# One table of order for a fused attention and MoE kernel on one Trainium2 core

## The chip, the cores and the metric

The kernel runs on one core of a Trainium2 chip. The metric is the device time of one execution in microseconds (us); a profiled execution also gives a span, from its first to its last instruction. The engines are named as the profile names them: PE (TensorE, matmuls; PEld its weight loads), DVE (VectorE), ACT (ScalarE), POOL (GpSimd), SP (SyncE, here a queue of transfers). POOL and ACT issue transfers too. Each engine works through its own list in order, and waits on semaphores for the others.

## What is computed

```python
# q, k, v: 8 batches, 8 heads, 576 positions, 64 wide; w1, w2: 512 x 1024; w_out: 1024 x 512
scores = scale * np.matmul(q, k.transpose(0, 1, 3, 2))
mask = block_i >= block_j            # blocks of 64 positions
scores = np.where(mask, scores, -1000000000.0)
...
attn = np.exp(scores)
attn = attn / (np.sum(attn, axis=-1, keepdims=True) + 1e-09)
attn_out = np.matmul(attn, v)
x = attn_out.transpose(0, 2, 1, 3).reshape(4608, 512)
h1 = x @ w1
h2 = x @ w2
g = np.maximum(h1, h2)
return g @ w_out
```

## The kernel before

**Attention.** The 64 heads are worked on as 32 pairs; two pairs make a group (16 groups), and two groups a batch. q and k of a group are loaded in fp32 (L121), cast to bf16 (L161), and transposed on PE (L525), with copies out of PSUM (L533). From group 6 on, k takes another way: four casting transfers on POOL's queue (L138) and two transposing transfers on SP (L147). v is loaded with a cast on POOL's queue (L165). Scores of a pair (L544, the causal corner at L562) fill PSUM tiles of 2 x 512, two of them in all; ACT takes the exponential (L568, a corner at L624), POOL writes zeros over masked corners (L573), PE multiplies by v with a column of ones for the sums (L652), and DVE divides (L658, L659). The result goes to `xT`, by PE transposes (L690, L692) for groups 0 to 3 and 15, and by transposing transfers on SP (L670) for the others. For the first four pairs the scores come in smaller pieces (`burst_p`, `burst_q1` to `burst_q3`), so that the first 256 tokens are ready early.

**MoE.** max(h1, h2) is written as h2 + relu(x (w1 - w2)). So g holds relu(x D) with D = w1 - w2 (`diff_w`, L191; `h_unit`, matmul L244, relu L250 on ACT or L252 on DVE), and the output is x M + g w_out with M = w2 w_out (`bT_unit` transposes w2, L261; `m_unit`, L272 and L277). Output tiles of 512 tokens by 512 columns are made as two by two blocks by seven products (`product`, L390; Strassen's scheme in Winograd's form), with sums of the weights (`weight_sums`, L358), sums S1 to S4 of the rows of x and g (`row_sums`, L364: one part of 512 columns from x, one of 1024 from g), and sums of products (`after`, L415 to L449), which stores the output too (L409). All of these sums run on DVE. S1 to S4 lie in one set of buffers, of which the x part alternates with a second set (`xsum`).

Spans of tokens are 256, 320, then 512 each and 448 at the end. Since the first two make 576, later spans start at an odd multiple of 64, and POOL copies the 64 columns of g left over to the next span (L236).

**What sets the order.** The program is written out by hand for the first batch. MoE work is a list of units (`plan`), each with the tokens that it needs and a cost; `fill(n)` takes n units of cost from the first entry that is ready, and the loop over groups calls it between the pieces of attention. `pool_work` places POOL's casts and loads; with `gated=True` a load of q or k is preceded by a memset of one column on POOL (L120), which waits for the buffer in SP's stead. The weights come on POOL's queue, a quarter of w1 and w2 at a time (L185, L187), then w_out in halves (L197). The last span's products go in the order of `LAST` (L390), and `warm_up` issues matmuls on zeros (L514).

Of the kernel before, what the change touches and what calls it, by code (L numbers as in the profile page):

```python
# [14 lines left out]
def kernel(  # L15
# [10 lines left out]
    nc = tc.nc  # L26
# [31 lines left out]
    QCUT = 256  # L58

    def a_col(p, c, t):  # L60
        if p >= HP:
            return CB[c] + t * P
        late = t * P >= QCUT
        return t * P + {
            0: 384 - QCUT if late else 0, 1: 704 - QCUT if late else 256 - P,
            2: 1024 - QCUT, 3: 1408 - 3 * P, 4: 1344 - 4 * P,
        }[c]


    SPAN = 512  # L70
    spans = [(0, QCUT), (QCUT, S - QCUT)]
    spans += [(t0, min(SPAN, NTOK - t0)) for t0 in range(S, NTOK, SPAN)]
    NSPAN = len(spans)


    FAST = 2
    carry = [t0 % P for t0, _ in spans]
    tiles = [(carry[i] + w) // P for i, (_, w) in enumerate(spans)]
# [34 lines left out]
    def load_qk(g, queues, gated=False):  # L113
        b, u = divmod(g, GPB)
        for nm, src, queue in (("q", q, queues[0]), ("k", k, queues[1])):
            if queue is None or by_dma(nm, g):
                continue
            raws[nm, g] = t = raw.tile([P, 2, RPP * D], FP32, name=f"{nm}raw")
            if gated:
                nc.gpsimd.memset(t[:, 0, :1], 0.0)  # L120
            queue.dma_start(  # L121
                out=t[:],
                in_=src[b, 4 * u:4 * u + 4].rearrange(
                    "(s h) (p t) d -> (h p) s (t d)", h=2, t=RPP),
            )

    T_DMA = {nm: 6 for nm in "k"}
    blk_n = {}

    def by_dma(nm, g):  # L130
        return g >= T_DMA.get(nm, NG)

    def load_blocks(nm, g):
        b, u = divmod(g, GPB)
        blk_n[nm, g] = n = raw.tile([P, S // BLK, 2, D], BF16, name=f"{nm}b", tag=f"{nm}raw")
        for h in range(2):
            for s in range(2):
                nc.gpsimd.dma_start(  # L138
                    out=n[h * BLK:(h + 1) * BLK, :, s],
                    in_=(q if nm == "q" else k)[b, 4 * u + 2 * s + h].rearrange(  # L140
                        "(j p) d -> p j d", p=BLK),
                )

    def transpose_blocks(nm, g):
        n = blk_n.pop((nm, g))
        for h in range(2):
            nc.sync.dma_start_transpose(  # L147
                out=(qT_r if nm == "q" else kT_r)[(2 * g + h) % NT].rearrange(
                    "q (j p) -> q j p", p=BLK),
                in_=n[h * BLK:(h + 1) * BLK].rearrange("p j s d -> p (j s d)"),  # L150
            )

    def cast(nm, g, parts):
        if by_dma(nm, g):
            return
        t = raws[nm, g].rearrange("p s (t d) -> p t s d", d=D)
        if (nm, g) not in qk_n:
            qk_n[nm, g] = qkn.tile([P, RPP, 2, D], BF16, name=f"{nm}n")
        n = qk_n[nm, g]
        for copy, j0, j1 in parts:  # L160
            copy(out=n[:, j0:j1], in_=t[:, j0:j1])  # L161
# [19 lines left out]
    def load_w(j, which=(0, 1)):  # L181
        fs = slice(j * WB, (j + 1) * WB)
        if 0 in which:
            w1_raw[j] = wraw.tile([P, NDM, WB], FP32, name="w1raw")
            nc.gpsimd.dma_start(out=w1_raw[j][:], in_=w1r[:, :, fs])  # L185
        if 1 in which:
            nc.gpsimd.dma_start(out=w2_sb[j], in_=w2r[:, :, fs])  # L187

    def diff_w(j):
        fs = slice(j * WB, (j + 1) * WB)  # L190
        nc.vector.tensor_sub(d_sb[:, :, fs], w1_raw[j][:], w2_sb[j])  # L191
# [8 lines left out]
    dve, pool, act = nc.vector.tensor_copy, nc.gpsimd.tensor_copy, nc.scalar.copy  # L200
    SP, ACT = nc.sync, nc.scalar
    warm = small.tile([P, 1], FP32, name="warm")
    load_qk(0, (SP, ACT))
    nc.vector.memset(warm[:], 0.0)
    zeros = wpool.tile([P, SPAN], BF16, name="zeros")
    nc.vector.memset(zeros[:], 0.0)
    nc.scalar.activation(out=warm[:], in_=warm[:], func=AF.Exp)
    load_qk(1, (SP, SP))
    load_qk(2, (SP, None))
    make_identity(nc, ident)  # L210
    for r in range(NV):
        nc.vector.memset(vv_r[r][:, :, :, D:D + 1], 1.0)
        nc.vector.memset(vv_r[r][:BLK, NCH - 1, :, :], 0.0)
    for r in range(NA):
        nc.vector.memset(aT_r[r][:, :, AW:], 0.0)
    for r in range(NT):
        nc.vector.memset(kz_r[r][:, BLK:2 * BLK], 0.0)
    cast("q", 0, ((dve, 0, 7), (pool, 7, RPP)))
    cast("k", 0, ((act, 0, 5), (dve, 5, RPP)))
    for c in range(2):  # L220
        load_v(0, c)
    load_w(0, (0,))
    cast("q", 1, ((pool, 7, RPP),))
    cast("k", 1, ((pool, 0, 7),))
    load_w(0, (1,))


    done_tokens = [0]
    g_tiles = {}

    def h_unit(i, f):
        if f == 0:
            g_tiles[i] = g_pool.tile([P, NFF, SPAN + BLK], BF16, name="g")
            if carry[i]:
                end = carry[i - 1] + spans[i - 1][1]
                nc.gpsimd.tensor_copy(  # L236
                    out=g_tiles[i][:, :, :carry[i]],
                    in_=g_tiles[i - 1][:, :, end - carry[i]:end])
        g = g_tiles[i]
        t0, w = spans[i]  # L240
        m = carry[i]
        pt = ps_m.tile([P, SPAN], FP32, name="ps_h", tag="m")
        for c in range(NDM):
            nc.tensor.matmul(  # L244
                pt[:, :w], d_sb[:, c, f * P:(f + 1) * P], xT[:, c, t0:t0 + w],
                start=(c == 0), stop=(c == NDM - 1),
            )
            if c == NDM - 1:
                if i >= FAST and on_act(i, f):
                    nc.scalar.activation(out=g[:, f, m:m + w], in_=pt[:, :w], func=AF.Relu)  # L250
                else:
                    nc.vector.tensor_scalar_max(g[:, f, m:m + w], pt[:, :w], 0.0)  # L252
                if i in (1, *range(FAST, NSPAN)) and f in X_SUMS:
                    row_sums(i, X_SUMS[f], 0)
            yield

    def bT_unit(j):
        pt = ps_m.tile([P, 2, NDM, P], BF16, name="ps_bT", tag="m")
        for i in range(2):
            for c in range(NDM):  # L260
                nc.tensor.transpose(pt[:, i, c, :], w2_sb[j][:, c, i * P:(i + 1) * P], ident[:])  # L261
                if i == 1 and c == NDM - 1:
                    (act if j % 2 else dve)(
                        out=bT_sb[:, 2 * j:2 * j + 2, :],
                        in_=pt.rearrange("p i c d -> p i (c d)"))
                yield

    def m_unit(i, c):
        ds = slice(i * WH, (i + 1) * WH)
        pt = ps_m.tile([P, WH], FP32, name="ps_M", tag="m")  # L270
        for f in range(NFF):
# [4 lines left out]
            if f == NFF - 1:  # L276
                nc.vector.tensor_copy(out=m_sb[:, c, ds], in_=pt[:])  # L277
                for k in M_SUMS[NDM * (1 - i) + c]:
                    weight_sums(k)
            yield  # L280

    def y_terms(i, s):
        g = g_tiles[i]
        t0 = spans[i][0] - carry[i] + s * P
        return [(xT[:, c, t0:t0 + P], m_sb[:, c]) for c in range(NDM)] + [
            (g[:, f, s * P:(s + 1) * P], wo_sb[:, f]) for f in range(NFF)]

    def y_unit(i, s):
        t0 = spans[i][0] - carry[i] + s * P
        py = ps_m.tile([P, d_model], FP32, name="ps_y", tag="m")  # L290
        terms = y_terms(i, s)
        for n, (lhs, rhs) in enumerate(terms):
            nc.tensor.matmul(
                py[:], lhs, rhs, start=(n == 0), stop=(n == len(terms) - 1),
            )
            if n == len(terms) - 1:
                y = y_pool.tile([P, d_model], FP32, name="y")
                nc.vector.tensor_copy(out=y[:], in_=py[:])
                nc.sync.dma_start(out=out[t0:t0 + P, :], in_=y[:])
            yield  # L300

    def y_last(i, s):
        t0 = spans[i][0] - carry[i] + s * P
        for m, w, copy, queue in ((0, 256, act, SP), (256, P, dve, SP), (384, P, act, ACT)):
            py = ps_m.tile([P, w], FP32, name="ps_y", tag="m")
            terms = y_terms(i, s)
            for n, (lhs, rhs) in enumerate(terms):
                nc.tensor.matmul(
                    py[:], lhs, rhs[:, m:m + w], start=(n == 0), stop=(n == len(terms) - 1),
                )  # L310
                if n == len(terms) - 1:
                    y = y_pool.tile([P, d_model], FP32, name="y")
                    copy(out=y[:, :w], in_=py[:])
                    queue.dma_start(out=out[t0:t0 + P, m:m + w], in_=y[:, :w])
                yield

# [12 lines left out]
    def a_parts(i, row, half):  # L329
        j, r = (row, 0) if i == 1 else (i, row)  # L330
        g, t0 = g_tiles[j], spans[j][0] - carry[j] + 2 * r * P
# [605 lines left out]
```

## Time and profile before

| what | before |
|---|---|
| device time, median of 3 runs | 247.88 us (247.6 to 254.31) |
| device time of the profiled execution | 247.61 us |
| its span | 245.8 us |
| mean granted PE clock | 0.997 |
| busy: PE, DVE, ACT, POOL | 234.4, 185.4, 143.8, 129.6 us |
| first h matmul | 18.6 us |
| first matmul of M, first of the seven products | 38.3 us, 52.2 us |
| last attention matmul | 204.5 us |

Busy time is the union of an engine's instructions. A matmul's record runs from its start until its result is written, so matmuls overlap and a busy PE is not PE at its peak. In the groups, a line gives the line of the kernel, the engine, the operation, output<-inputs and their shape, the count, then busy us and mean ns of one, then idle time ahead of them and what ended it. A few matmul records are missing.

### The profile page before, as it was taken

Reading aid. Unit: us, or ns where it says so; the run is one execution under the profiler, and the core shown is the slowest. Engines: PE = TensorE matmul, PEld = TensorE weight load, DVE = VectorE, ACT = ScalarE, POOL = GpSimd, SP = SyncE. Lnnn points to the kernel's source line nnn. Section 1 sums busy time; section 2 is a strip of 40 time slices with the busy share of each in tenths; the row PEclk is TensorE's granted clock in tenths of the full one; section 3 lists DMA queues with packets and bytes.
Section 4 is the critical chain, followed back from the end, with each engine's and each line's share of the span. In section 5 each row is a group of like instructions: output and inputs, shape, how many; then the busy total and the mean of one; then the engine's idle time right before and its main releaser. Section 6 shows DMA issues by size and latency. Waiting matters only on the chain.

```text
span 245.8 us, 7595 instructions
## 1 busy us (share of the span) xinstructions
PE 234.4 (95%) x3093; PEld 167.3 (68%) x3109; DVE 185.4 (75%) x395; ACT 143.8 (58%) x200; POOL 129.6 (53%) x294
## 2 busy tenths in 40 slices
PE   7689899999999999999999999999999999999993
PEld 2347666688865886588558755875587578567782
DVE  4976989999677958795879587957785788526573
ACT  2888871677677748673867386748673730462200
POOL 1996952669959584948593859485621210010000
PEclk9999999999999999999999999999999999999998
DMA  6999999579999999999999999999994321301125
GB/s 233 318 206 306 231 278 195 172 137 188 153 196 180 168 163 222 184 201 183 244 227 130 208 164 272 122 223 193 134 138 97 100 39 45 131 0 43 47 86 172
DMA packets 108867, 41.33 MB, mean 168 GB/s; under 512 B 89248, under 2 KB 102688, under 8 KB 108832
## 3 DMA queue, kind: packets, MB, share of 16 engines
q0 software_dynamic: 65952, 11.87, 69.4%
q1 hardware_dynamic: 42464, 28.32, 51.7%
q10 hardware_dynamic: 416, 0.66, 0.8%
q8 instruction: 24, 0.39, 0.7%
q14 instruction: 11, 0.09, 0.1%
HBM read 34.60 MB, written 9.44 MB: 179 GB/s over the span
## 4 chain that ended last, share of the span: by engine, by line
PE 87%; DVE 7%; ACT 4%; issue 1%; ACTq 0%
PE ps_p L390 35%; PE ps_h L244 24%; PE ps_o L652 11%; PE ps_s L544 9%; PE ps_w L514 3%; ACT aT L568 3%; PE ps_qT L525 2%; DVE sums L358 2%; DVE sums L364 1%; DVE g L252 1%; DVE m_sb L277 1%; PE ps_s L562 1%; PE ps_xe L690 1%; PE ps_bT L261 1%; DVE qT L533 1%
## 5 line engine op out<-in xcount | busy, mean ns | idle before, releaser
L568 ACT ACTIVATE aT<-ps_s 128x1024 bf16<-128x1024 f32 (+2 forms) x100 | 95.7, 994 | 32.1 <-PE ps_s L544 24.0
L244 PE MATMUL ps_h<-xT,d_sb 128*128 128x512 bf16 (+3 forms) x307 | 68.0, 357 | 1.0 <-DVE d_sb L191 0.3
L573 POOL MEMSET aT<- 64x128 bf16 x124 | 21.8, 200 | 52.8 <-ACT aT L568 51.9
L244 PEld LDWEIGHTS <-d_sb 128*128 128x128 bf16 x320 | 29.7, 98 | 26.7 <-issue 2.2
L652 PEld LDWEIGHTS <-aT 128*128 128x128 bf16 x960 | 37.2, 98 | 6.9 <-issue 0.8
L652 PE MATMUL ps_o<-vv,aT 128*128 128x65 bf16 x960 | 39.8, 194 | 0.3 <-DVE xp L659 0.3
L250 ACT ACTIVATE g<-ps_h 128x512 bf16<-128x512 f32 (+1 forms) x40 | 23.3, 587 | 23.3 <-PE ps_h L244 22.3
L165 POOL DMA_DIRECT2D vv<-in_v_dram x40 | 33.9, 857 | 1.1 <-issue 0.9
L252 DVE TENSOR_SCALAR g<-ps_h 128x512 bf16<-128x512 f32 (+2 forms) x40 | 23.6, 594 | 13.1 <-PE ps_h L244 12.8
L659 DVE TENSOR_TENSOR xp<-ps_o,rec 128x256 bf16<-128x256 f32 (+1 forms) x64 | 31.4, 491 | 2.2
L544 PE MATMUL ps_s<-qT,kT 64*128 64x64 bf16 (+6 forms) x344 | 31.3, 280 | 1.8 <-ACT kT L533 0.7
L390 PE MATMUL ps_p<-sums,bT_sb 128*128 128x256 bf16 x216 | 32.8, 273 | 0.0
L390 PEld LDWEIGHTS <-bT_sb 128*128 128x128 bf16 x288 | 27.5, 98 | 4.5 <-issue 1.4
L138 POOL DMA_DIRECT2D kb<-in_k_dram x40 | 29.5, 765 | 0.0
L533 ACT COPY qT<-ps_qT 128x576 bf16<-128x576 bf16 (+1 forms) x17 | 10.3, 614 | 23.2 <-PE ps_qT L525 23.2
L390 PEld LDWEIGHTS <-g 128*128 128x128 bf16 x220 | 19.8, 98 | 4.8 <-issue 2.8
L390 PE MATMUL ps_p<-wo_sb,g 128*128 128x256 bf16 (+1 forms) x148 | 22.7, 270 | 0.0
L161 POOL CAST qn<-qraw 128x1152 bf16<-128x1152 f32 (+1 forms) x16 | 17.1, 1067 | 5.1 <-DMA qraw<-in_q_dram 5.1
L544 PEld LDWEIGHTS <-kT 64*128 64x128 bf16 x344 | 12.2, 94 | 10.5 <-issue 5.1
L658 DVE RECIPROCAL rec<-ps_o 128x4 f32<-128x4 f32 (+1 forms) x64 | 11.8, 184 | 6.8 <-PE ps_o L652 6.8
L236 POOL COPY g<-g 128x512 bf16<-128x512 bf16 x8 | 5.9, 733 | 20.6 <-ACT g L250 20.3
L364 DVE TENSOR_TENSOR bT_sb<-g 128x1024 bf16<-128x1024 bf16 x18 | 12.4, 688 | 5.4 <-ACT g L250 4.8
(90 smaller groups left out, 326.1 us busy)
## 6 DMA issues: line engine op xcount, KB each, us to landing
qraw<-in_q_dram SPq DMA_DIRECT2D x16, 576.0 KB, 6.0
out_dram<-y SPq DMA_DIRECT2D x35, 256.0 KB, 3.9
vv<-in_v_dram POOLq DMA_DIRECT2D x32, 128.0 KB, 7.3
kraw<-in_k_dram SPq DMA_DIRECT2D x5, 576.0 KB, 7.4
kb<-in_k_dram POOLq DMA_DIRECT2D x40, 72.0 KB, 6.8
w1raw<-in_moe_w_dram POOLq DMA_DIRECT2D x4, 512.0 KB, 8.8
xT<-in_moe_w_dram POOLq DMA_DIRECT2D x4, 256.0 KB, 9.2
wo_sb<-in_moe_w_out_dram POOLq DMA_DIRECT2D x2, 512.0 KB, 10.9
```

The source lines that it names most:

```text
L138: nc.gpsimd.dma_start(out=n[h * BLK:(h + 1) * BLK, :, s], in_=(q if nm == "q" else k)[b, 4 * u + 2 * s + h].rearrange("(j p) d -> p j d", ...
L161: copy(out=n[:, j0:j1], in_=t[:, j0:j1])
L165: nc.gpsimd.dma_start(out=vv_r[b % NV][P - rows:, c, :, :D], in_=v[b, :, c * P:c * P + rows, :].rearrange("h p d -> p h d"),)
L244: nc.tensor.matmul(pt[:, :w], d_sb[:, c, f * P:(f + 1) * P], xT[:, c, t0:t0 + w], start=(c == 0), stop=(c == NDM - 1),)
L250: nc.scalar.activation(out=g[:, f, m:m + w], in_=pt[:, :w], func=AF.Relu)
L252: nc.vector.tensor_scalar_max(g[:, f, m:m + w], pt[:, :w], 0.0)
L390: nc.tensor.matmul(pt[:, q0:q0 + w], lhs[c][:, s * P:(s + 1) * P], rhs[c][:, m:m + w], start=(c == 0 and q0 == 0), stop=(c == 5 and q0 + w ...
L544: nc.tensor.matmul(ps[:, hh, col:col + w], kT[r, k0:k0 + P], qT[r, q0:q0 + w], start=True, stop=True,)
L568: nc.scalar.activation(out=aT_r[p % NA][:, :, a0:a0 + w], in_=ps[:, :, :w], func=AF.Exp, scale=scale,)
L573: (eng or nc.gpsimd).memset(aT_r[p % NA][BLK:, :, a0:a0 + BLK], 0.0)
L652: nc.tensor.matmul(po[:, gi, hh, :], a[:, hh, a0:a0 + P], vv[:, c, h0 + 2 * hh, :], start=(mm == 0), stop=(mm == n_mm - 1),)
L659: nc.vector.tensor_mul(xp[:, :, ts[0]:ts[0] + n, p % 2].rearrange("q s t d -> q t s d"), po[:, :, :, :D], rec[:, :n].to_broadcast([P, n, 2 ...
```

## The change

The order is no longer made while the program is built: a table of some 950 tokens is read from the front, and each token issues one step (`step`). `S4_2` is score tile 2 of pair 4; `E4_2:P` its exponential with the masks on POOL; `A4a`/`N4a` the AV product and its division, first (a) or second (b) part; `Cq3a:P` a cast; `Tq3`, `cq3_1:D` transposes and a copy out; `Lq3`, `u0`, `v0`, `o0` loads of q, w1, w2, w_out; `K6_0`, `J6_0`, `I4_0`, `V1_3` the k and x transposing ways and v; `B`, `M`, `D`, `W` the steps of the weights; `R5_21:P` row sum S2 of span 5, part 1 (g); `H4` four h matmuls, `Y4` eight matmuls of products. The letter after the colon names the engine.

- Spans: nine of 512 tokens, each by the seven products; the left-over copy of g and `xsum` are gone.
- All scores of all pairs are made in full tiles (three of 512 columns), where the first four pairs had smaller pieces.
- w2, w_out and M come ahead of w1; w1 is loaded on SP's queue. The loads of q and k on SP have a gate only where the table names an engine (`Lk2:P`, `Lk3:P`, `u0:D`, `Lq10:P`).
- The engine of each cast, copy, mask and sum is chosen in the table. All four `diff_w`, three of eight `weight_sums` and 40 of 72 `row_sums` go to POOL (21 of the 40 are of 1024 columns, 19 of 512); 64 of 128 masks go to DVE, and several casts and copies change between POOL, DVE and ACT.
- The division (`normalize`) is a step of its own and may come later than the AV product.
- PE's list changes from 3109 to 3069 matmuls; the warm-up matmuls are 29 in both.

```diff
-    spans = [(0, QCUT), (QCUT, S - QCUT)]
-    spans += [(t0, min(SPAN, NTOK - t0)) for t0 in range(S, NTOK, SPAN)]
-    NSPAN = len(spans)
+    NSPAN = NTOK // SPAN
...
-    def load_w(j, which=(0, 1)):
-            nc.gpsimd.dma_start(out=w1_raw[j][:], in_=w1r[:, :, fs])
+    def load_w1(j, gate=None):
+        w1_raw[j] = t = wraw.tile([P, NDM, WB], FP32, name="w1raw")
+        if gate is not None:
+            gate.memset(t[:, 0, :1], 0.0)
+        nc.sync.dma_start(out=t[:], in_=w1r[:, :, j * WB:(j + 1) * WB])
...
-    def diff_w(j):
-        nc.vector.tensor_sub(d_sb[:, :, fs], w1_raw[j][:], w2_sb[j])
+    def diff_w(j, eng):
+        eng.tensor_sub(d_sb[:, :, j * WB:(j + 1) * WB], w1_raw[j][:], w2_sb[j])
...
-    def row_sums(i, n, k):
+    def row_sums(i, n, k, eng):
+        sums_slots()
+        sub, add = eng.tensor_sub, eng.tensor_add
...
-        for m in G_SUMS.get(n, ()):
-            row_sums(i, m, 1)
...
+    SCHEDULE = """
+        z14 mk:D mz2:P Cq0a:P V0_2 ma:D Ck0a:A V0_1 V0_3 Cq0b:D Tq0 Ck0b:A mo1:D Lq1:N Cq1a:A Tk0 ck0_1:A
+        ck0_0:D cq0_1:A cq0_0:D z6 S0_1 V0_0 V0_4 Z1 S1_1 Lk1:N Ck1a:D Ck1b:A Z0 Tk1 ck1_0:D v2 z2 S0_0 E1_1:P
...
+        E2_1:D B1:D S3_0 E3_0:P X0:DA S2_2 E2_2:P B2:D B0:D A2a N2a B3:A Lk2:P A3b A2b Lq2:N A3a u0:D Lk3:P
+        Ck2a:P M02:A M00:A N2b M01:A Ck2b:A N3a N3b X1:AD Cq2a:P M12:D D0:P M11:D Tk2 ck2_0:D Z4 Cq2b:A u1:N
+        u2:N ck2_1:A D1:P Z5 V1_3 M03:D D2:P Tq2 cq2_0:A M13:A Ck3a:A Ck3b:D H2 Lq3:N Cq3a:P H1 M10:A cq2_1:D
...
+        S16_1 Tq9 H1 cq9_0:A H4 A13b K10_2 H4 Y5 V4_3 N13b I6_1 Y1 A15a
...
+        Y1 R7_21:P R7_40:D Y5 H3 Y4 H4 Y2 H2 R7_41:D H1 Y1 H1 Y5 H1 Y5 H1 Y4 H5 R8_11:D Y1 R8_30:D Y5 R8_31:P
+        Y2 R8_10:P R8_20:P R8_40:D Y4 R8_21:P Y4 R8_41:D Y32
+    """
...
+        elif kind == "D":
+            diff_w(n[0], ENGINE[o])
+        elif kind == "R":
+            row_sums(n[0], *divmod(n[1], 10), ENGINE[o])
+        elif kind == "H":
+            for _ in range(n[0]):
+                next(h_work)
+        elif kind == "Y":
+            for _ in range(2 * n[0]):
+                next(y_work)
```

## The prediction

> **What bounds the kernel now.** I read the page's first two parts, then busy time by stage, then the chain of waits, then the groups of POOL by shape, then the timeline and the DMA issues. From the page and its slices:
>
> ```profile
> span 245.8 us, 7595 instructions
> PE 234.4 (95%) x3093; PEld 167.3 (68%) x3109; DVE 185.4 (75%) x395; ACT 143.8 (58%) x200; POOL 129.6 (53%) x294
> PE   7689899999999999999999999999999999999993
> POOL 1996952669959584948593859485621210010000
> ```
>
> By stage (start:end, length, then busy us and count of each engine, granted clock, DMA):
>
> ```profile
> 6.00:24.00 18.00, 14.74 (x287) 9.03 (x287) 14.02 (x34) 14.73 (x23) 15.47 (x29) 1.00 1.43 277
> 36.00:72.00 36.00, 35.03 (x590) 27.25 (x591) 33.05 (x72) 21.78 (x29) 22.92 (x54) 1.00 1.32 169
> 72.00:190.00 118.00, 117.53 (x1575) 83.44 (x1582) 89.48 (x184) 77.84 (x105) 76.38 (x176) 1.00 1.66 184
> ```
>
> PE leaves 0.5 of 118 us idle from 72 us on; what it loses, it loses before. The chain of waits gives its price per matmul:
>
> ```profile
> 207.09 3.38 PE ps_p L390 x30
> 210.95 7.18 PE ps_h L244 x33
> ```
>
> In the dense stretches the timeline has a matmul start every 0.109 us (256 columns), 0.216 (512), 0.056 (128), 0.029 (65, attention times values); products over 64 rows run in pairs, at half of that each; a change from 128 rows to 64 costs 0.096 and back 0.085. Priced so, all of PE's list is 227.0 us before and 226.8 us after the change. It is a good price: from 71.5 us to the last matmul the list says 168.0 us, the trace took 170.0. So the span is 1.2 (first matmul) + 227.0 + 13.4 lost + 4.2 (last sum and store), and 11.4 of the 13.4 are lost before 71.5 us. Only those can be won, and anything that stops PE later is a loss.
>
> **The change part by part, with no cost of its own.** Nine equal spans in place of 256, 320, seven of 512 and 448 tokens, and full score tiles: PE's price falls by 0.2 us, eight POOL copies of g (0.73 each) go, 16 exponentials of the first four pairs become 12: all beside PE. Masks, casts and q/k copies change engine; DVE, ACT and POOL keep idle time in each stage above. w1 goes from POOL's queue to SP's: four issues fewer on POOL, 3.1 us in all. Loads of q on SP lose their gate, so SP itself waits for the buffer, with output stores and transposes queued behind; with three buffers per tensor that buffer was cast three groups earlier (a group takes 12 us in the chain), so I cost it at nothing.
>
> **The head, up to the first h matmul.** It needs w1's first quarter, loaded after w2 and w_out. On ACT: the casts of k0 end at 7.6 (first row of ACT 6.25, 0.73 and 0.6), then one cast of q1, two copies (0.64 each) and one cast of k1: 10.3. Then twelve exponentials of four pairs, which the timeline shows at 3.46 us for four, so 0.9 each, with four short ones and a copy: the twelfth ends at 23. POOL masks it, and only then issues the gate memset for group 2's loads on SP; w1's first quarter is third there, at 24.5. From before:
>
> ```profile
> 21.48 3.46 ACT L568 ACTIVATE aT<-ps_s 128x1024 bf16<-128x1024 f32 x4
> ...
> w1raw<-in_moe_w_dram POOLq DMA_DIRECT2D x4, 512.0 KB, 8.8
> wo_sb<-in_moe_w_out_dram POOLq DMA_DIRECT2D x2, 512.0 KB, 10.9
> ```
>
> So it lands at about 33 (24.5 + 8.8). PE meanwhile has, from 25.5, the last three AV tiles, M (eight matmuls a unit, 0.87 us) and transposes, 9 us: 34.5, if w_out (issued at 17, 10.9 to land: 28) is there soon enough. First h at 35. What is left on PE's list: 288 h 62.2, 762 product matmuls 82.4, 840 AV 24.4, scores 19.2, transposes 5.0, one M 0.9, 45 changes of rows 8.1: 202.1. Without any stop: 35 + 202.1 + 4.2 = 241.3, against 245.8. The head's gain is 4.5 us, because M fills idle PE time.
>
> **What it adds: POOL as a second adder.** Before, every row sum, weight sum and w1 - w2 runs on DVE. After, POOL gets the four w1 - w2, three weight sums, and 40 of 72 row sums. No row of before shows POOL adding two tensors. Its nearest rows have one input:
>
> ```profile
> L165 POOL DMA_DIRECT2D vv<-in_v_dram x40 | 33.9, 857 | 1.1 <-issue 0.9
> L138 POOL DMA_DIRECT2D kb<-in_k_dram x40 | 29.5, 765 | 0.0
> L573 POOL MEMSET aT<- 64x128 bf16 x124 | 21.8, 200 | 52.8 <-ACT aT L568 51.9
> L161 POOL CAST qn<-qraw 128x1152 bf16<-128x1152 f32 x14 | 16.2, 1160 | 0.6 <-DMA qraw<-in_q_dram 0.6
> L551 POOL COPY kz<-kT 128x128 bf16<-128x128 bf16 x28 | 8.9, 340 | 8.2 <-DMA qraw<-in_q_dram 6.2 <-DMA kT<-kb 1.1
> L161 POOL CAST qn<-qraw 128x256 bf16<-128x256 f32 x2 | 0.8, 417 | 4.5 <-DMA qraw<-in_q_dram 4.5
> ```
>
> The two casts give 0.83 ns an element and 0.2 us fixed. Low end: a second input is free, 1.05 us for 1024 and 0.63 for 512. High end: each input is read at the cast's rate, 1.9 and 1.05. I take the high end: a POOL that needs 0.83 ns for one stream shows no spare reading, and the next rows show POOL and DVE in each other's way as soon as DVE has two inputs. The same sum of 512 columns took 0.41 alone and 0.96 beside a POOL cast, until that cast ended:
>
> ```profile
> 148.76 0.96 DVE L364 TENSOR_TENSOR xsum<-xsum,xT 128x512 bf16<-128x512 bf16 x1
> 149.64 0.41 DVE L364 TENSOR_TENSOR xsum<-xT 128x512 bf16<-128x512 bf16 x1
> ...
> 148.29 1.15 POOL L161 CAST qn<-qraw 128x1152 bf16<-128x1152 f32 x1
> ```
>
> [...]
>
> **Where POOL stops PE.** POOL's list is in order, and its first w1 - w2 can't start before the load lands, 33. From there to the cast of q for group 9, which PE's transposes wait for, it holds: 17 v loads 14.6, 19 k loads 14.5, 14 key pads 4.8, 27 masks 5.4, 9 casts 9.1, small 0.7, together 49.0; and 9 sums of 1024 and 6 of 512. Low: 49.0 + 9 x 1.05 + 6 x 0.63 = 62.3, done at 95.3. High: 49.0 + 17.1 + 6.3 = 72.4, done at 105.4. PE's own price from first h to those transposes is 59.3, so it is there at 94.3. Hold: 1.0 low, 11.2 high. Before that point the casts of q and k for group 5 and a row sum of span 0 pass part of it on; after it POOL's list is lighter than PE's, and nothing more is held until the ends of the late spans. There POOL's sums stand right ahead of their readers:
> - Span 6: from the last h, PE has 2.7 us up to the sixth product's use of S2; the relu (0.7) and two POOL sums of 1024 follow each other. High 4.5, stop 1.8; low 0.1.
> - Span 7: 4.9 us for relu, 1024, 512, 1024. High 5.6, stop 0.7; low none.
> - Span 8: S3's buffer comes free at span 7's last product; POOL then does 1024, 512, 512, 1024 before the sixth product can go on, with two products (2.8 us) on PE in between. High 5.9, stop 3.1; low 3.4, stop 0.5. Before, DVE did these with no loss on PE.
>
> Together high 5.6, low 0.6. Sum: 241.3 + 11.2 + 5.6 = 258.1 us of span. The profiled execution took 247.61 for a span of 245.8, so 1.8 more: 259.9, **260 us**. It agrees with the median 247.88 of the runs to 0.1%.
>
> **Rivals.** (1) POOL's second input is free: 241.3 + 1.0 + 0.6 + 1.8 = 244.7, within 2% (a difference under 2% is about what a measurement of this kernel can't tell from no change). For it: POOL is idle 47% of the span. Against it: the cast's rate. (2) The other sign, faster: M ahead of h fills the head, and POOL holds nothing. It needs sums of 1024 at about 1 us and w1's first quarter 2 us earlier, as the fastest w1 load of before (8.05 to 14.49, 6.4 us) would have it: first h at 33, 239.3 of span, 241.1, 2.7% faster. It decides where h starts before 35 and POOL's list to group 9 takes under 61 us. Against it: behind w2, w_out and two loads of group 2 the queues are full. (3) The change doesn't fill the head: w_out's second half took 12.9 us to land in before (25.19 to 38.08), and now v and w2 are in front of it; M starts at 30 instead of 25.5 and h at 39. By itself that is 4 us on rival 1: 249, no change. With POOL at the high end POOL hides it.
>
> **How the numbers follow.** POOL at the high end or beyond 0.63, its own range 252 to 268 (a price between the ends at the bottom; at the top each POOL sum also waits for a DVE sum). Rival 1 and rival 3 together 0.22, at 243 to 250. Rival 2: 0.15. All of the first case but its top, and rivals 1 and 3 from 242 up, make the range 242 to 268, leaving out rival 2 and a little above. Faster by over 2% 0.15, within 2% 0.22, slower 0.63.
>
> **What would show it.** In the profile after: the mean of POOL's TENSOR_TENSOR of 1024 (1.9 expected; 1.05 is rival 1); first h matmul at 35; POOL over 90% busy from 35 to 105 and PE's idle time there ended by POOL (qn, kn, sums); in the last 12 us PE stops for about 3 us ahead of the sixth product. Wrong: POOL's sums near 1 us with PE dense from 50 us on, or PE stopped by DMA, DVE or ACT instead.

## The result: 284.1 us, 14% slower, and the profile after

The changed kernel took 284.1 us (median of 4 runs, 282.93 to 284.54), the kernel before 248.8 beside it: a ratio of 1.144 [1.136, 1.152]. Ratios leave out executions over 1.5% above the fastest of their kernel, such as the one of 254.31 us of the kernel before. The profiled execution took 282.93 us, its span is 281.2. So the direction of the forecast came true, and its size did not: 36 us were lost (over the 247.88 of the kernel before that the prediction used), not 12.

From the page of the changed kernel, the span, the busy times, and the slices of PE, POOL and the granted clock:

```profile
span 281.2 us, 7430 instructions
PE 241.7 (86%) x3043; PEld 163.2 (58%) x3069; DVE 179.0 (64%) x393; ACT 150.9 (54%) x211; POOL 183.8 (65%) x254
PE   8689783889987887999999999999899779989573
POOL 3950499999994899798929916966564660560720
PEclk9999999999999999999999999999999979999978
```

PE no longer has its unbroken row of nines. POOL is at nine tenths or more from 35 to 84 us. And in two slices near the end, both 7, the granted clock is below full (the last slice, an 8, is below full in the kernel before too); the PEclk row of the kernel before has a 9 in every slice but the last.

By stage, with the columns as before (start:end, length, busy us and count of PE, PEld, DVE, ACT, POOL, then clock, DMA share, GB/s):

```profile
6.00:24.00 18.00, 14.79 (x271) 9.29 (x273) 12.07 (x32) 16.31 (x23) 12.12 (x22) 1.00 1.38 175
36.00:72.00 36.00, 28.81 (x457) 18.43 (x458) 30.07 (x57) 25.10 (x35) 35.00 (x45) 1.00 1.04 175
72.00:190.00 118.00, 107.75 (x1391) 71.99 (x1404) 81.42 (x189) 72.47 (x99) 90.82 (x139) 1.00 1.42 163
```

From 36 to 72 us PE does 457 matmuls where it did 590, and POOL has 1 us free of 36. From 72 to 190 us PE has 10 us idle where it had 0.5.

POOL's costliest groups, each shape apart:

```profile
L262 POOL TENSOR_TENSOR bT_sb<-g 128x1024 bf16<-128x1024 bf16 x9 | 19.6, 2176 | 19.5 <-PE ps_p L282 10.6 <-ACT g L187 5.4 <-issue 1.9
...
L262 POOL TENSOR_TENSOR sums<-xT 128x512 bf16<-128x512 bf16 x11 | 12.9, 1172 | 11.6 <-PE ps_p L282 11.0 <-POOL aT L423 0.2
...
L161 POOL TENSOR_TENSOR d_sb<-w1raw,xT 128x1024 bf16<-128x1024 f32 x4 | 8.5, 2131 | 2.1 <-DMA w1raw<-in_moe_w_dram 2.0
```

A sum of 1024 columns takes POOL 2.12 to 2.18 us and one of 512 takes 1.15 to 1.17 (means of the groups): a little over the high end of the prediction (1.9 and 1.05), three times DVE's 0.69 and 0.41 in the kernel before. The 47 sums take POOL 81.3 us in all.

The waits say who stops PE (engine, line, waited for: us in total, times, longest):

```profile
PE ps_p L282 <- POOL bT_sb L262: 6.8, 3, 3.8
...
PE ps_h L181 <- DVE g L189: 4.6, 2, 2.7
...
PE ps_qT L376 <- POOL qn L131: 3.1, 4, 1.6
...
DVE sums L262 <- POOL sums L262: 3.1, 2, 2.0
...
PE ps_p L282 <- POOL sums L262: 2.6, 1, 2.6
...
DVE sums L254 <- POOL d_sb L161: 1.9, 1, 1.9
```

POOL stops PE itself, and it stops DVE, which stops PE. (Among the waits left out here, PE waits 2.8 us for loads of v, in three stops.) How the second works is seen in the timeline of the changed kernel, from 42 us (start, length, instruction, and in brackets the idle time ahead and its releaser):

```profile
42.08 0.91 DVE L254 TENSOR_TENSOR sums<-sums,m_sb 128x512 bf16<-128x512 bf16 x1 [1.93 <-POOL d_sb L161]
...
42.91 0.68 DVE L189 TENSOR_SCALAR g<-ps_h 128x512 bf16<-128x512 f32 x1
...
43.64 1.02 PE L181 MATMUL ps_h<-xT,d_sb 128*128 128x512 bf16 x4 [1.82 <-DVE g L189]
44.19 2.13 POOL L161 TENSOR_TENSOR d_sb<-w1raw,xT 128x1024 bf16<-128x1024 f32 x1
...
44.93 1.94 DVE L254 TENSOR_TENSOR sums<-wo_sb 128x1024 bf16<-128x1024 bf16 x1
46.27 1.80 POOL L135 DMA_DIRECT2D vv<-in_v_dram  x2
46.79 1.37 DVE L254 TENSOR_TENSOR sums<-m_sb 128x512 bf16<-128x512 bf16 x1
...
48.08 0.68 DVE L189 TENSOR_SCALAR g<-ps_h 128x512 bf16<-128x512 f32 x1
...
48.81 0.38 PE L181 MATMUL ps_h<-xT,d_sb 128*128 128x512 bf16 x1 [2.74 <-DVE g L189]
```

A weight sum on DVE first waits 1.93 us for POOL's w1 - w2 (the sums lie in the buffers that w1 was loaded into). Two more take 1.94 and 1.37 us where alone they take 0.67 and 0.41, the first beside POOL's sum, the second beside POOL's DMA issues. The relu stands behind them in DVE's list, and PE behind the relu: 1.8 and 2.7 us.

To see where time is lost I use the prediction's price list: the *lateness* of a matmul is its start less the price of all matmuls ahead of it on PE's list. It grows only where PE waits or runs slower. All variants of the changed kernel have the same list on PE, so they can be compared point by point:

| lateness, us | predicted | after | all sums on DVE | one copy on POOL | copies on DVE |
|---|---|---|---|---|---|
| first h matmul (price 24.9) | 10.1 | 10.8 | 12.2 | 10.0 | 12.1 |
| first q transpose of group 9 (83.9) | 21.5 | 28.7 | 21.4 | 18.1 | 20.0 |
| last matmul (226.8) | 27.1 | 49.8 | 35.7 | 24.3 | 28.5 |

The last three columns are experiments 1, 2 and 5 below. The kernel before ends 14.6 late by its own list.

### The profile page after: what moved, and what is told of

It is laid out like the page before. It is cut to its first block, busy times and chain, and to the rows that moved or that the text cites. A ratio compares the mean times of both kernels' runs of the same rounds, so it can differ in the third digit from the quotient of the medians.

```text
span 281.2 us, 7430 instructions
## 1 busy us (share of the span) xinstructions
PE 241.7 (86%) x3043; PEld 163.2 (58%) x3069; DVE 179.0 (64%) x393; ACT 150.9 (54%) x211; POOL 183.8 (65%) x254
## 5 line engine op out<-in xcount | busy, mean ns | idle before, releaser
L418 ACT ACTIVATE aT<-ps_s 128x1024 bf16<-128x1024 f32 x96 | 95.1, 1025 | 26.3 <-PE ps_s L394 24.9
L181 PE MATMUL ps_h<-xT,d_sb 128*128 128x512 bf16 x265 | 70.9, 380 | 8.6 <-DVE g L189 4.6
L187 ACT ACTIVATE g<-ps_h 128x512 bf16<-128x512 f32 x40 | 24.0, 599 | 54.8 <-PE ps_h L181 50.3
L282 PE MATMUL ps_p<-sums,bT_sb 128*128 128x256 bf16 x216 | 35.6, 284 | 6.8 <-POOL bT_sb L262 6.8
L262 POOL TENSOR_TENSOR bT_sb<-g 128x1024 bf16<-128x1024 bf16 x9 | 19.6, 2176 | 19.5 <-PE ps_p L282 10.6
L394 PE MATMUL ps_s<-qT,kT 64*128 64x512 bf16 (+4 forms) x320 | 31.4, 288 | 1.0 <-ACT aT L418 0.7
L189 DVE TENSOR_SCALAR g<-ps_h 128x512 bf16<-128x512 f32 x32 | 22.0, 686 | 13.0 <-PE ps_h L181 13.0
L423 POOL MEMSET aT<- 64x128 bf16 x64 | 11.6, 205 | 26.8 <-ACT aT L418 25.6
L282 PE MATMUL ps_p<-sums 128*128 128x256 bf16 x108 | 21.9, 286 | 3.4 <-POOL sums L262 2.6
L475 DVE RECIPROCAL rec<-ps_o 128x4 f32<-128x4 f32 (+1 forms) x64 | 11.7, 183 | 14.9 <-PE ps_o L464 14.4
L262 POOL TENSOR_TENSOR sums<-xT 128x512 bf16<-128x512 bf16 x11 | 12.9, 1172 | 11.6 <-PE ps_p L282 11.0
L282 PEld LDWEIGHTS <-sums 128*128 128x128 bf16 x144 | 13.6, 101 | 8.8 <-POOL sums L262 3.4
L394 PEld LDWEIGHTS <-kT 64*128 64x128 bf16 x320 | 11.2, 94 | 10.1 <-issue 7.6
```

What stands on the lines that cost most here:

```text
L181: nc.tensor.matmul(pt[:], d_sb[:, c, f * P:(f + 1) * P], xT[:, c, t0:t0 + SPAN], start=(c == 0), stop=(c == NDM - 1),)
L187: nc.scalar.activation(out=g[:, f], in_=pt[:], func=AF.Relu)
L189: nc.vector.tensor_scalar_max(g[:, f], pt[:], 0.0)
L262: op(s_parts(i, n)[k], get(x)[k], get(y)[k])
L282: nc.tensor.matmul(pt[:, q0:q0 + w], lhs[c][:, s * P:(s + 1) * P], rhs[c][:, m:m + w], start=(c == 0 and q0 == 0), stop=(c == 5 and q0 + w ...
L394: nc.tensor.matmul(ps[:, hh, col:col + w], kT[r, k0:k0 + P], qT[r, q0:q0 + w], start=True, stop=True,)
```

## Experiments

The ratios are to the kernel before on the same chip, which took 247.7 to 247.8 us.

**1. All 47 sums to DVE.** The theory was the prediction's: POOL is the cause. The rival: the order of the table is.

```diff
-  D0:P ... R0_10:P ... W6:P ... R8_21:P      (47 tokens)
+  D0:D ... R0_10:D ... W6:D ... R8_21:D
```

> All 47 two-input sums that the table gives to POOL (w1 - w2, weight sums, row sums) are done by DVE instead; the order of the table stays. POOL theory (POOL's price for a sum, 2.1 us against DVE's 0.7, is what holds PE): nearly all of the 35 us comes back, 246 us (242 to 252), no stop of PE ended by a sum, the granted clock without a slow stretch after 10 us. Rival, order theory (the table's order itself makes PE wait for DVE, ACT and loads, whoever adds): half comes back at most, 262 us or more.

268.9 us, 1.083 [1.079, 1.087]: 15 us come back of 36. POOL's theory fails by its number (246). The rival's number holds (262 or more), but it does not show the order alone at fault, since DVE now has 47 more sums: ahead of products PE waits 6.5 us for DVE's sums, in eight stops. From 36 to 72 us DVE is busy for 33.62 of 36 us. The kernel before had 33.05 there with PE idle for 1 us, so a full DVE by itself is not the reason; what stands ahead of the relus and copies that PE needs is.

```profile
36.00:72.00 36.00, 31.92 (x473) 20.87 (x475) 33.62 (x70) 27.27 (x38) 24.81 (x44) 0.96 1.28 188
```

**2. Each POOL sum a copy of its first input.** The instructions and their places stay; the second input, the arithmetic and a wait for the second input alone are left out (S4 is A - S2, so a copy of A no longer waits for S2). The same edit is made for w1 - w2.

```diff
+        one = lambda o, a, b: eng.tensor_copy(out=o, in_=a)
+        sub, add = (one, one) if eng is nc.gpsimd else (eng.tensor_sub, eng.tensor_add)
```

> POOL's 47 sums are replaced by POOL copies of their first input alone, so that the second input is left out of the sums; all else is as in the changed kernel. POOL theory: the copy takes 1.1 us for 1024 columns instead of 2.1, POOL is about 31 us less busy, and the time falls by two thirds of what was lost, to 252 us (247 to 260); DVE's sums still wait beside it. Order theory: 270 us or more.

258.5 us, 1.043 [1.038, 1.048]. The copies take about half, on POOL's rows of this kernel:

```profile
L259 POOL COPY bT_sb<-g 128x1024 bf16<-128x1024 bf16 x15 | 16.1, 1079 | 20.1 <-PE ps_p L284 13.9 <-ACT g L187 4.1 <-issue 1.9
...
L259 POOL COPY sums<-xT 128x512 bf16<-128x512 bf16 x13 | 8.2, 638 | 10.9 <-PE ps_p L284 10.5
```

All 47 together take 41.4 us of POOL instead of 81.3, and the execution is 25.6 us shorter. So the second input, with what waits for it, costs 25.6 of the 36 us. But this is also the case that the first rival of the prediction assumed (1.05 and 0.63), and it priced it at 244.7.

**3. The 15 POOL sums of the last three spans to DVE** (tokens `R6_10:P` to `R8_21:P`).

> Only the row sums of spans 6, 7 and 8 move from POOL to DVE (15 of them). POOL theory: the three stops ahead of the sixth products (4.0, 1.5 and 4.6 us) and the two slow stretches of the clock after them (1.7 us each) go, 13 us together: 271 us. Order theory: DVE, which has the sums of products as well, makes PE stop in their place, and less than 5 us comes back.

276.4 us, 1.113 [1.108, 1.118]: 7.7 us come back, between the two theories (13, and less than 5). In their place PE now waits 4.9 us in four late stops for DVE's sums.

**4. w1 - w2 and the weight sums to DVE** (`D0` to `D3`, `W5` to `W7`).

> Only the four w1 - w2 and the three weight sums move from POOL to DVE. POOL theory: PE's lateness between the first h matmul and the first AV of pair 4 (7.3 us) shrinks by 4 us, of which the later hold of POOL's list takes none back, since POOL's list gets 14 us shorter before group 9: 275 us (270 to 280). Order theory: no change, 284 us, or slower since DVE stands in front of the relus of span 0.

280.7 us, 1.131 [1.126, 1.136]: 3.4 us come back, again between the two (9, and none). The first h matmul then starts at 37.2 instead of 35.6, since DVE waits 3.23 us for w1 with copies of M behind.

After these four, two theories were left: that the rest is still the sums, by their place right ahead of their readers; or that the order of masks, casts and loads costs by itself.

**5, 6 and 7. How much the table costs without dear sums.** In 5, all weight and row sums are copies of their first input, on DVE, and w1 - w2 is a true subtraction there; in 6, all masks are on POOL besides; in 7, the sums are true sums on DVE, as in 1, with all masks on POOL.

```diff
-        op(s_parts(i, n)[k], get(x)[k], get(y)[k])
+        nc.vector.tensor_copy(out=s_parts(i, n)[k], in_=get(x)[k])     (5 and 6)
...
-  E0_1:D ... E30_2:D        (6 and 7: 49 tokens)
+  E0_1:P ... E30_2:P
```

> The changed kernel, with every weight sum and row sum replaced by a copy of its first input, on DVE (the second input and the arithmetic are left out; w1 - w2 stays a subtraction, on DVE). The order of all else is the table's. Sum theory (what the table loses, 36 us, it loses at the sums, on whichever engine they stand): PE loses about what it lost in the kernel before: 246 to 251 us. Table theory (loads, casts, masks and copies in the table's order stop PE by themselves): not under 255 us, since copies on POOL gave 258.5.

> As the kernel with every sum a copy of its first input on DVE (the second input is left out), and all masks on POOL besides. Mask theory: 3 to 6 us less than that kernel. Sum theory: the same as it within 1.5 us. If both theories fall, it stays over 255 us, and loads (v, k) or the table's order on PE are what is left.

> The changed kernel with all 47 two-input sums on DVE, and all masks on POOL, which the sums leave free (as in the kernel before). Mask theory (49 score tiles have their masks on DVE, which waits there 13.8 us for exponentials with relus, copies and sums queued behind): 258 to 264 us, against 268.9 with the masks as in the table. Sum theory (DVE is full of sums where PE waits, masks are idle time that costs nothing): 267 to 270 us.

261.5 us, 1.053 [1.048, 1.059]; 267.0 us, 1.079 [1.074, 1.084]; 272.4 us, 1.098 [1.094, 1.102]. The sum theory's number (246 to 251) fails in the first: with copies of 0.3 to 0.5 us in the place of all sums the table still loses 14 us. That does not clear the sums of all of it. PE still waits 3.5 us in four stops for these copies, and 2.5 us at 34.7 for a copy of M that stands behind w1 - w2 on DVE; PE's granted clock is 0.50 from 34.0 to 40.8, which costs up to 3.0 us more. The mask theory fails with the wrong sign (3 to 6 us less in 6, 258 to 264 us in 7 were forecast): masks on POOL cost 5.4 us more (6 against 5) and 3.5 more (7 against 1). A mask waits for its exponential, and on POOL the casts, loads of v and key pads wait behind it; in the second of the three kernels PE's waits for masks are 3.0 us in three stops. In the kernel before, with its masks on POOL, PE is idle 0.5 us of 118.

**8. The test from the other side: the kernel before with the change's 40 row sums on POOL.**

```diff
+        if (i, n, k) in ON_POOL:        # the 40 of the table
+            op = nc.gpsimd.tensor_add if n == 1 else nc.gpsimd.tensor_sub
         op(s_parts(i, n)[k], get(x)[k], get(y)[k])
```

> The kernel before, with the 40 row sums that the change gives to POOL run on POOL, and nothing else changed. Price theory (a two-input sum of 2.18 us on POOL, and DVE sums that wait beside it, cost PE wherever they are placed): all 47 sums were worth 15 us in the changed kernel, the seven of the weights 3.4 of them, so some 12 us here too: 260 us (255 to 266). Place theory (only the table's place for them, right ahead of their readers, makes them cost; before's list has slack, POOL is idle 47% of its span): 248 to 251 us.

284.8 us, 1.149 [1.146, 1.153]: 37 us from the sums alone, in an order that had lost 2 us after 72 us. Both theories fail (260; 248 to 251). That it is as much as the change lost is chance: there 11 us of the loss are left with cheap sums (2), and here part of it is the clock, which was granted at 0.50 for 23.9 us in four stretches that begin in stops or behind them (up to 9 us, for the 17.6 us of it in which PE has work). The timeline of this kernel shows one of its stops from the start:

```profile
79.24 1.15 POOL L161 CAST qn<-qraw 128x1152 bf16<-128x1152 f32 x1
80.32 2.43 POOL L165 DMA_DIRECT2D vv<-in_v_dram  x3
...
82.73 2.96 POOL L138 DMA_DIRECT2D kb<-in_k_dram  x4
85.63 1.23 POOL L366 TENSOR_TENSOR sums<-sums,xT 128x512 bf16<-128x512 bf16 x1
86.89 0.42 DVE L366 TENSOR_TENSOR sums<-xT,sums 128x512 bf16<-128x512 bf16 x1 [6.50 <-POOL sums L366]
...
87.92 0.66 PE L536 MATMUL ps_qT<-ident,qn 64*128 64x64 bf16 x17 [5.93 <-DVE xp L670]
```

S4 on DVE needs S2 from POOL. POOL first casts and issues seven loads (6.5 us), so DVE waits 6.50 us for a sum of 1.23. The division stands behind DVE's sum, PE's transposes wait for the PSUM buffer that the division reads: 5.93 us. Two more stops of this kind are 5.29 and 3.82 us, where DVE waits 5.86 and 7.00 us for a POOL sum; and PE itself waits 5.8 us in four stops for POOL's sums of 1024.

**9. Nine POOL sums that no other sum waits for.** The kernel before with only the x part of S3 on POOL.

```diff
+        if (n, k) == (3, 0):
+            op = nc.gpsimd.tensor_sub
```

> The kernel before, with one row sum of each span on POOL: the 512 columns of x in S3, which no other sum reads. Place theory (with 40 sums on POOL the kernel before lost 37 us because DVE's sums wait for POOL's, S2 for S1 and S4 for S2, with the division behind them): 247 to 250 us, no loss. Price theory (each us of POOL sum costs its share: 9 x 1.17 us of the 40 sums' 68 us): 253 us (251 to 256).

248.0 us, 0.9995 [0.995, 1.004]: free. PE's line on this kernel's page is that of before, and its POOL sums take no less than elsewhere:

```profile
PE 234.6 (95%) x3093; PEld 167.2 (68%) x3109; DVE 184.0 (75%) x386; ACT 143.8 (58%) x200; POOL 140.7 (57%) x303
...
PE   7689899999999999999999999999999999999993
```

```profile
L366 POOL TENSOR_TENSOR sums<-xT 128x512 bf16<-128x512 bf16 x5 | 6.4, 1273 | 0.3
...
L366 POOL TENSOR_TENSOR xsum<-xT 128x512 bf16<-128x512 bf16 x4 | 5.0, 1260 | 0.2
```

So it is not a price per microsecond of POOL: a sum of 1.26 us with slack ahead of its reader costs nothing. The nine differ from the forty of experiment 8 in their readers, but in their number and length too; which of these made them free is not shown.

**10. Is it POOL's time or what the instruction does to DVE?** Each POOL sum of the changed kernel as two copies, one per input.

```diff
+        two = lambda o, a, b: (eng.tensor_copy(out=o, in_=b), eng.tensor_copy(out=o, in_=a))
+        sub, add = (two, two) if eng is nc.gpsimd else (eng.tensor_sub, eng.tensor_add)
```

> The changed kernel with each of the 47 two-input sums on POOL replaced by two copies, one of each input (the arithmetic is left out). POOL is then as long at each of them as in the changed kernel (1.06 x 2 for 1024 columns, 0.63 x 2 for 512, from the kernel with one copy), but never reads two inputs at once. Time theory (what costs is that POOL is late, whatever its instruction is): 280 to 286 us, like the change. Lock theory (what costs is that DVE's sums can't run beside POOL's, 0.41 to 0.69 us become 1.9 to 2.3): 268 to 274 us.

282.6 us, 1.141 [1.135, 1.147]. The 94 copies take POOL 83.1 us (81.3 for the sums), and the time is that of the change. One copy 258.5, two copies 282.6, the sum 284.1: what counts is how long POOL takes at these places, not that one of its instructions reads two inputs. The lock (DVE's sums taking longer beside POOL) is not parted from it by this: DVE's sums still take longer beside the copies (0.82 us in place of 0.98 for the seven `sums<-xT,sums`, 0.41 alone).

**11. DVE's own 37 sums as copies of one input, POOL's as they are.**

```diff
+        one = lambda o, a, b: eng.tensor_copy(out=o, in_=a)
+        sub, add = (eng.tensor_sub, eng.tensor_add) if eng is nc.gpsimd else (one, one)
```

> The changed kernel with the 37 row and weight sums that the table gives to DVE replaced by copies of their first input (the second input and the arithmetic are left out), POOL's sums as they are. Lock theory: DVE no longer waits beside POOL, its relus and copies come on time from 36 to 60 us, where 5 us of PE's stops were ended by a relu: 270 to 277 us. Time theory: POOL is as late as before, 279 to 284 us.

280.6 us, 1.134 [1.127, 1.141]. By its numbers it speaks for time, but it does not tell what it was made to tell: the copies on DVE wait beside POOL as well. The timeline of this kernel:

```profile
43.71 2.11 POOL L161 TENSOR_TENSOR d_sb<-w1raw,xT 128x1024 bf16<-128x1024 f32 x1
43.75 2.37 DVE L249 COPY sums<-wo_sb 128x1024 bf16<-128x1024 bf16 x1
45.78 1.80 POOL L135 DMA_DIRECT2D vv<-in_v_dram  x2
46.03 1.67 DVE L249 COPY sums<-m_sb 128x512 bf16<-128x512 bf16 x1
```

Copies that take 0.42 and 0.28 us alone (experiment 5) took 2.37 and 1.67. How many microseconds the lock is worth in the change stays open.

**12. Sums on DVE, only w1 - w2 left on POOL** (tokens `R` and `W` to DVE).

> The changed kernel with the row sums and weight sums on DVE, and only the four w1 - w2 left on POOL. If what the version with all 47 on DVE paid at its head is DVE waiting for w1 with M's copies queued behind (PE stopped 2.2 us there, and the clock fell to a half for 3.4 us after it): first h matmul at 35.5 instead of 37.0, no half clock at 36, 264 to 267 us. If not: 268 to 270 us, as with all of them on DVE.

273.8 us, 1.104 [1.097, 1.111]: over both forecasts, and worse than with w1 - w2 on DVE too, by 4.9, though the first h matmul starts at 36.0 instead of 37.0. At group 9 PE is 26.0 us late, against 21.4 in experiment 1. One stop and what follows it explain most of that, in the timeline of this kernel:

```profile
44.57 2.11 POOL L161 TENSOR_TENSOR d_sb<-w1raw,xT 128x1024 bf16<-128x1024 f32 x1
...
46.72 0.42 DVE L254 TENSOR_TENSOR sums<-m_sb,sums 128x512 bf16<-128x512 bf16 x1 [3.01 <-POOL d_sb L161]
47.06 0.68 DVE L189 TENSOR_SCALAR g<-ps_h 128x512 bf16<-128x512 f32 x1
...
47.80 0.62 PE L376 MATMUL ps_qT<-ident,qn 64*128 64x64 bf16 x18 [3.95 <-DVE g L189]
```

It is the chain of the change at 42 us, twice as long: POOL's last w1 - w2, the weight sum on DVE that writes into its buffer, the relu behind, PE. A half clock (0.50 granted) of 6.8 us follows it (48.7 to 55.5).

## Why the prediction was right in direction and wrong in size

Point by point, by its own steps:

- **The price of PE's list, the kernel before**: used as it was for all comparisons above, and it held in the stretches without stops.
- **The head**: right. M at 25.3 (25.5 predicted), w1's first quarter there at 33.5 (33), first h at 35.6 (35). The third rival's late w_out did not happen. Of the 4.5 us that the head was to win, 3.8 were there at the first h matmul (10.8 us late for 10.1), and were lost after it.
- **The price of a POOL sum**: right in kind, the high end, and 10 to 15% under the size (2.12 to 2.18 for 1.9, 1.15 to 1.17 for 1.05).
- **Where POOL stops PE, up to group 9**: predicted hold 11.2 at the high price and 1.0 at the low one, a difference of 10.2. Measured, 17.9 (28.7 - 10.8) and, with the cheap copies, 8.1: a difference of 9.8. POOL's part of this stage was right in size, in part by luck: its fifteen sums there took about 13 us longer than the copies, of which 9.8 reached PE, where the prediction let its 10.2 through in full. And the way was not only the casts of q (3.1 us by all four waits): 4.6 us came by DVE's relus, behind sums that waited for POOL. The prediction had the lock between the two engines only as a delay of POOL's sums, at the top of its range; no run shows each of them waiting for a DVE sum: three of the 47 in the changed kernel took 0.2 to 0.4 us over the usual 2.12 and 1.15 (2.33, 2.53 and 1.33), beside a sum of DVE that had begun first. It is DVE's sums, and what queues behind them, that were held: eleven that began beside a POOL sum took 0.44 to 2.34 us, against 0.41 to 0.69 alone.
- **After group 9**: "nothing more is held until the ends of the late spans" failed. PE lost 21.1 us after it where 5.6 were forecast, and 6.2 with the cheap copies where 0.6 were: POOL's part is 14.9, not 5.0. The stops of spans 6, 7 and 8 were 4.0, 1.5 and 4.6 (1.8, 0.7 and 3.1 forecast), the half clock behind two of them cost 3.4 us, and the rest is in many stops of up to 1.5 us, which the prediction did not have. In the changed kernel's timeline of the last span:

```profile
261.41 2.53 POOL L262 TENSOR_TENSOR bT_sb<-g 128x1024 bf16<-128x1024 bf16 x1 [10.59 <-PE ps_p L282]
...
263.90 1.33 POOL L262 TENSOR_TENSOR sums<-xT 128x512 bf16<-128x512 bf16 x1
...
265.32 1.15 POOL L262 TENSOR_TENSOR sums<-sums,xT 128x512 bf16<-128x512 bf16 x1
266.42 2.11 POOL L262 TENSOR_TENSOR bT_sb<-bT_sb,g 128x1024 bf16<-128x1024 bf16 x1
...
266.52 0.39 PE L282 MATMUL ps_p<-sums 128*128 128x256 bf16 x2 [2.64 <-POOL sums L262]
...
268.59 0.88 PE L282 MATMUL ps_p<-sums,bT_sb 128*128 128x256 bf16 x4 [1.68 <-POOL bT_sb L262]
```

  The chain was named rightly (1024, 512, 512, 1024) and takes 7.1 us, not 5.9; both its x part and its g part stop PE. And PE's stops brought the half clock (below), twice, up to 1.7 us each, which the prediction did not have.
- **"With no cost of its own"**: this is the step that failed most. The parts that were costed at nothing, beside PE (masks, casts and copies on other engines, loads without gates, all in the table's order), were to leave 242.9 us of span with POOL at its low price, as in rival 1. Experiment 2 is that case, and its span is 255.6: 12.7 us more, 7.1 of it before group 9 and 5.6 after it. From the first h on PE loses 14.3 us there, half of it in stops of 0.5 us and more. From the page of this kernel:

```profile
span 255.6 us, 7423 instructions
...
L181 PE MATMUL ps_h<-xT,d_sb 128*128 128x512 bf16 x265 | 70.7, 379 | 3.0 <-DVE g L189 1.8
L466 PE MATMUL ps_o<-vv,aT 128*128 128x65 bf16 x960 | 37.9, 194 | 2.8 <-DMA vv<-in_v_dram 1.4
L284 PE MATMUL ps_p<-sums,bT_sb 128*128 128x256 bf16 x216 | 33.8, 273 | 1.7 <-POOL bT_sb L259 1.7
```

  The larger stops, in lateness, were for relus on DVE (0.8 and 1.3), for v (1.3), for row sums on POOL (1.3, 0.6 and 0.8), and for a mask, a q copy and a sum of products (0.5 to 0.6 each); the other half is in smaller ones. Not all of it belongs to this step: the row sums' 2.6 us are POOL's ends of the late spans again (0.6 forecast), and both relus stand behind weight sums on DVE, one of which had waited 0.77 us for POOL's copy of w1. So the parts costed at nothing cost at most 12.7 us, and some 8 if the stops behind sums (4.7) are taken off. I had looked at idle time per stage and concluded that the engines had room. What mattered is how much lies between each step and its reader, and I never measured that slack in the table.

So the miss of 23.1 us of span (281.2 for 258.1) is 12.7 that are there even with cheap sums on POOL, and 10.4 from the sums' price, 25.6 where 15.2 were forecast.

**What the experiments show together.** Shown: that POOL's time at its sums costs 24 to 26 of the 36 us in this table (2 and 10); that 40 such sums cost 37 us in the old order too, where DVE's sums wait for POOL's (8), and that nine that no other sum reads cost nothing there (9); that DVE cannot take all the sums in this table either (1); that the table loses 11 to 14 us with cheap sums, on either engine (2 and 5). Not settled: how much of these 11 to 14 us is the order of masks, casts and loads, which of the small stops would go with which edit, and the share of the lock. No run here has the sums of the table taken out altogether, and none has the kernel before with its sums made cheap. None of the versions beats the kernel before.

## What to carry to other kernels

POOL, idle 47% of the time before, was no free adder: in experiment 8 DVE waited 6.50 us for a sum of 1.23 us that stood behind a cast and seven loads in POOL's list. So ask of each moved step what stands ahead of it there and who waits for it, not how busy the engine is. Keep dependent steps on one engine, or move only those whose readers are far away: nine such sums were free, and forty, many of them read by sums on the other engine, cost 37 us (the two differ in number and length too). And a new order of everything has to show its slack step by step; room per stage did not tell of it here.

## What the runs showed of the hardware that I had not expected

**A half clock behind some of PE's stops.** Three windows of the changed kernel: one around a stop of 3.8 us, the 3.4 us that begin 1.1 us after it, and 3.4 us more:

```profile
223.00:227.00 4.00, 0.27 (x3) 0.25 (x4) 0.79 (x2) 0.88 (x2) 3.86 (x4) 1.00 0.20 68
227.80:231.20 3.40, 3.40 (x43) 2.80 (x40) 2.38 (x7) 0.00 (x0) 1.49 (x1) 0.50 0.02 5
231.30:234.70 3.40, 3.35 (x40) 2.27 (x40) 1.15 (x3) 1.18 (x2) 0.00 (x0) 1.00 0.00 0
```

In the middle one PE has no idle time and a granted clock of 0.50: a matmul of 256 columns starts every 0.213 us instead of 0.109. The record of the clock changes at 227.83 and back at 231.24, 3.41 us later. The second stretch of the changed kernel, 268.79 to 272.20, is as long. The kernel before with 40 sums on POOL has four of them (3.4 to 6.8 us each, 23.9 together); the version with one copy on POOL, whose longest stop after the head is 1.3 us, has none (mean granted clock 1.00). The first stretch followed a stop of 3.8 us, the second followed stops of 2.6 and 1.7 us with two matmuls between them, and one at 222.78 in experiment 12 followed a single stop of 2.0 us. The same stop, of 2.0 us at the same product, had no half clock behind it in experiment 1, where the one slice below full is that of 33 to 40 us. What decides is not shown.

**DVE beside POOL.** In the changed kernel eleven sums on DVE began while a two-input sum was at work on POOL. They took 0.44 to 2.34 us, where sums of their sizes take 0.41 and 0.69 alone, and each of them ended only after POOL's sum: by 0.28 to 0.29 us (the seven of 512 columns) or 0.55 to 0.56 (the four of 1024). In experiment 12 one of 512 columns took 2.91 us, from 40.47, and ended 0.95 after POOL's sum and 0.30 after the cast that followed it there. In experiment 11 the copy at 43.75 took 2.37 and ended 0.30 after POOL's sum, so DVE was held with one input too, where the prediction had named two. POOL's DMA issues are another matter: the 24 two-input sums on DVE that overlapped these alone (20 in the kernel before, 4 in the changed one) took 0.41 to 0.43 us and 0.68 to 0.69, as alone. The two slow ones shown above (1.37 us at 46.79 in the change, 1.67 at 46.03 in experiment 11) are exceptions, and why they were slow is not shown.
